# An attention and gated-MLP kernel: batch 0 loaded as rows and transposed on the tensor engine, loads reordered, and the numerators moved one period later

## The chip, the core and the metric

The kernel runs on one core of a Trainium2 chip. A core has a tensor engine (PE, with PEld for its weight loads), a vector engine (DVE), a scalar engine (ACT), GpSimd (POOL) and a sync engine (SP). Each engine works through its own queue of instructions in order and waits on semaphores. DVE and ACT read the tensor engine's results out of PSUM; POOL works in SBUF alone. DMAs are issued by SP, ACT and POOL. The metric is the device time of one execution in microseconds (us).

## The reference

There are B = 8 batches of H = 8 heads, S = 576 positions and D = 64 columns. Attention is linear, with a feature map of 128 columns and their negatives:

```python
proj = np.einsum('bhsd,df->bhsf', x, w_phi)
proj = proj - np.max(np.abs(proj), axis=-1, keepdims=True)
phi = np.concatenate([np.exp(proj), np.exp(-proj)], axis=-1)
kv = np.einsum('bhsf,bhsd->bhfd', k_p, v)
z = np.sum(k_p, axis=2)
num = np.einsum('bhsf,bhfd->bhsd', q_p, kv)
den = np.einsum('bhsf,bhf->bhs', q_p, z)[..., None] + 1e-06
x = num / den
```

The result, as rows of 512 columns, goes through a gated MLP: a causal convolution of five taps gives the gate, and the output is `(sigmoid(gate_pre) * (x @ w_val)) @ w_out`.

## The kernel before

The work goes batch by batch, and each batch is cut into units of one PSUM tile. All PSUM tiles have one tag with four buffers of two banks each (`ps2`), so at most four units are between PE and their readers.

*Loads.* `load_rows` (L70) brings k or q of a batch in transposed: POOL issues a DMA that casts the fp32 rows to bf16 in DRAM (L80, and L85 for the last 64 positions of each head), and SP issues a transposing DMA from there into `KT` or `QT` (L83, L86). `load_v` (L95) brings v in as fp32 rows, `VN` and `VNt`, on SP. `issue_after` places an issue behind a given instruction.

*Stage A, features.* `unit_k` (L210) projects 1024 columns of keys into `PK`; DVE takes the largest absolute value per position (L214), ACT makes the two exponentials `KTIL` (L219), and POOL negates the maxima (L223). `unit_vscale` (L225) makes `EK` from these on ACT (L229), and POOL multiplies v by it (`VT` L234, `VTt` L242, the sum's column L248). `unit_qmax` (L250) projects queries into `PQA` only for their maxima (L254). There are five units of each per batch, the last one half as wide.

*The mark between the stages.* `unit_mrows` (L259) transposes the maxima of q and makes `MQM` (L263), once per batch.

*Stage B.* `unit_qproj` (L268) projects the queries again with the maxima subtracted (`PQ`, L274 and L279), and ACT makes `QTIL` (L284) or, for the tail, `QTILt` (L301). `unit_kv` (L314) multiplies `KTIL` and `VT` into `KVPS` (L324, L334), copied to `KVSB` (L340). `unit_num` (L345) makes numerators and denominators (L355), which DVE divides into `XN` (L362, L364). `unit_xt` (L372) transposes these (L378) into `XT` (L383, L385).

*The MLP.* `unit_gate` (L390) is the convolution as matmuls with the diagonals `DIAG` (L397) and tanh (`GS`, L402), `unit_val` (L404) gives `VAL` (L409) and `GV` (L414), and `unit_out` (L419) gives `OUTp` (L426), which ACT copies to `OUTs` (L432) and SP stores (L440).

*The order.* Batch i's period begins with its stage A, merged by weights with gate and value units of batch i-1 (`merge`, L463). Then comes its stage B, written out by hand (L514 to L535), with the three output units of batch i-1 between. The numerators of batch i stand in its own stage B, behind its kv. So the MLP of a batch is one period behind its features. Batch 0 has its own `first_features` (L477), where `build_diag` (L169) stands behind the casts of q. A scheduler places the instructions of neighbouring units among each other, and each engine keeps the order it gives. The loads of batch i+1 are issued behind the first and second `VT` of batch i (L503, L506).

Of the kernel before, what the change touches and what calls it, by code (L numbers as in the profile page):

```python
# [9 lines left out]
AF = mybir.ActivationFunctionType  # L10
# [3 lines left out]
FP32 = mybir.dt.float32  # L14
BF16 = mybir.dt.bfloat16

B, H, S, D = 8, 8, 576, 64
F = 128
DM = 512
P = 128  # L20
E1 = D + 1
HALF = S // 2
NT = HALF - 2 * P
PAD = 2
TAIL = H * 2 * P
# [8 lines left out]
def kernel(  # L34
# [15 lines left out]
    nc = tc.nc  # L50

    const = ctx.enter_context(tc.tile_pool(name="const", bufs=1))
    dram = ctx.enter_context(tc.tile_pool(name="dram", bufs=3, space=bass.MemoryType.DRAM))
    qtp = ctx.enter_context(tc.tile_pool(name="qtp", bufs=3))
    vnp = ctx.enter_context(tc.tile_pool(name="vnp", bufs=2))
    featp = ctx.enter_context(tc.tile_pool(name="featp", bufs=2))
    smallp = ctx.enter_context(tc.tile_pool(name="smallp", bufs=2))
    vtp = ctx.enter_context(tc.tile_pool(name="vtp", bufs=2))
# [4 lines left out]
    ps2 = ctx.enter_context(tc.tile_pool(name="ps2", bufs=4, space=bass.MemoryType.PSUM))  # L63

    states = [_BatchState() for _ in range(B)]
# [23 lines left out]
    def load_k(st, parts=1):  # L89
        st.KT, st.k_xbars = load_rows(st, k, "KT", parts)  # L90

    def load_q(st, parts=1):
        st.QT, st.q_xbars = load_rows(st, q, "QT", parts)

    def load_v(st, anchor):  # L95
        b = st.b
        st.VN = vnp.tile([P, H, 4, D], FP32, name="VN")
        st.VNt = vnp.tile([P, 2, 2, D], FP32, name="VNt")
        with tc.issue_after(anchor):
            for hh in range(2):  # L100
                nc.sync.dma_start(
                    st.VN[:, 4 * hh:4 * hh + 4, :, :],
                    v[b, 4 * hh:4 * hh + 4, 0:4 * P, :].rearrange("h (p c) d -> p h (c d)", c=4),
                )
            for g in range(2):
                nc.sync.dma_start(
                    st.VNt[:, g, :, :],
                    v[b, 4 * g:4 * g + 4, 4 * P:S, :].rearrange("h (r t) d -> h r (t d)", t=2),
                )

    wtmp = const.tile([P, F], FP32, name="wtmp")
    nc.scalar.dma_start(wtmp[0:D, :], w_phi[:, :])
    nc.scalar.dma_start(wtmp[D:2 * D, :], w_phi[:, :])
    cw5 = const.tile([5, DM], FP32, name="cw5")
# [1 line left out]
    warm = const.tile([P, 1], FP32, name="warm")  # L116
    nc.vector.memset(warm[:, :], 0.0)
    nc.scalar.activation(warm[:, :], warm[:, :], AF.Exp)
    load_k(states[0], 2)


    ident_bf = const.tile([P, P], BF16, name="ident_bf")
# [46 lines left out]
    def build_diag():  # L169
        for dt in range(4):  # L170
            for tap in range(5):
                nc.gpsimd.tensor_scalar_mul(  # L172
                    DIAG[:, dt, tap, :], ident_f[:, :], cwTh[:, dt, tap:tap + 1],
                )

    def load_wval():
        nc.gpsimd.dma_start(WVAL[:, :, :], moe_w_val.rearrange("(dt p) j -> p dt j", p=P))
# [32 lines left out]
    def unit_k(st, u):  # L210
        PK = ps2.tile([P, 2, 4, F], FP32, name="PK", tag="b")
        nx = group_matmuls(st.KT, PK, u, 2)
        sl = slice(8 * u, 8 * u + 2 * nx)
        nc.vector.tensor_reduce(  # L214
            st.MK[:, 1, sl].rearrange("p (x t) -> p t x", t=2), PK[:, :, 0:nx, :],
            AX.X, ALU.max, apply_absolute_value=True,
        )
        for sgn in range(2):
            nc.scalar.activation(  # L219
                st.KTIL[:, sgn, sl, :].rearrange("p (x t) f -> p t x f", t=2),  # L220
                PK[:, :, 0:nx, :], AF.Exp, scale=1.0 - 2.0 * sgn,
            )
        st.neg_ops[u] = nc.gpsimd.tensor_scalar_mul(st.MK[:, 0, sl], st.MK[:, 1, sl], -1.0).ins  # L223
# [26 lines left out]
    def unit_qmax(st, u):  # L250
        PQ = ps2.tile([P, 2, 4, F], FP32, name="PQA", tag="b")
        n = group_matmuls(st.QT, PQ, u, 1)
        with nc.allow_low_precision("bf16 max"):
            nc.vector.tensor_reduce(  # L254
                st.MQb[:, :].rearrange("p (t s) -> p t s", t=2)[:, :, 4 * u:4 * u + n], PQ[:, :, 0:n, :],
                AX.X, ALU.max, apply_absolute_value=True,
            )

    def unit_mrows(st):  # L259
        MQT = ps2.tile([P, P], BF16, name="MQT", tag="b")  # L260
        nc.tensor.transpose(MQT[:, :], st.MQb[:, :], ident_bf[:, :])
        st.MQM = smallp.tile([P, 4, P], BF16, name="MQM")
        nc.vector.tensor_tensor(  # L263
            st.MQM[:, :, :], MQT[:, :].unsqueeze(1).to_broadcast([P, 4, P]),
            MASK[:, :].unsqueeze(2).to_broadcast([P, 4, P]), ALU.mult,
        )
# [152 lines left out]
    def unit_out(st, w):  # L419
        ob = out[st.b].rearrange("(i t) o -> t i o", t=2)  # L420
        cs = (2 * w, 2 * w + 1) if w < 2 else (4,)
        m = P if w < 2 else 2 * NT
        OUTp = ps2.tile([P, 2, DM], FP32, name="OUTp", tag="b")
        for n, c in enumerate(cs):
            for jt in range(4):
                nc.tensor.matmul(  # L426
                    OUTp[0:m, n, :],
                    st.GV[jt][:, :, :].rearrange("p t i -> p (t i)")[:, P * c:P * c + m],
                    WOUT[:, jt, :], start=(jt == 0), stop=(jt == 3),
                )  # L430
        OUTs = mlp.tile([P, 2, DM], FP32, name="OUTs", bufs=4)
        nc.scalar.activation(  # L432
            OUTs[0:m, 0:len(cs), :], OUTp[0:m, 0:len(cs), :], AF.Copy, scale=0.5,
        )
        for n, c in enumerate(cs):
            n0 = P * c
            while n0 < P * c + m:
                par, i0 = n0 // HALF, n0 % HALF
                k = min(P * c + m - n0, HALF - i0)
                nc.sync.dma_start(ob[par, i0:i0 + k, :], OUTs[n0 - P * c:n0 - P * c + k, n, :])  # L440
                n0 += k

    ORDER = (0, 2, 1, 3, 4)
# [5 lines left out]
    def units_features(st):  # L449
        us = []  # L450
        for u in ORDER:
            us.append((1.0, lambda u=u: k_scaled(st, u)))
            us.append((1.0, lambda u=u: unit_qmax(st, u)))
        return us

    def units_valgate(st):
        us = []
        for jt in range(4):
            us.append((1.2, lambda jt=jt: unit_gate(st, jt)))
            us.append((1.0, lambda jt=jt: unit_val(st, jt)))  # L460
        return us

    def merge(ua, ub):  # L463
        ta, tb = sum(w for w, _ in ua) or 1.0, sum(w for w, _ in ub) or 1.0
        ia = ib = 0
        fa = fb = 0.0
        while ia < len(ua) or ib < len(ub):
            if ib >= len(ub) or (ia < len(ua) and fa <= fb):
                fa += ua[ia][0] / ta
                ua[ia][1]()  # L470
                ia += 1
            else:
                fb += ub[ib][0] / tb
                ub[ib][1]()
                ib += 1

    def first_features(st):  # L477
        for u in ORDER:
            unit_k(st, u)
        with tc.issue_after(st.neg_ops[0]):  # L480
            load_q(st, 2)
        load_v(st, st.q_xbars[0])
        with tc.issue_after(st.cast):
            build_diag()
            load_wval()
        for u in ORDER:
            unit_vscale(st, u)
        for u in ORDER:
            unit_qmax(st, u)

    for i in range(B + 1):
        sa = states[i] if i < B else None
        sb = states[i - 1] if i > 0 else None
        if sa:
            alloc_A(sa)
            alloc_B(sa)
        if i == 0:
            first_features(sa)
        else:
            merge(units_features(sa) if sa else [], units_valgate(sb))  # L500
        if i + 1 < B:
            sn = states[i + 1]
            with tc.issue_after(sa.vt_ops[0]):  # L503
                load_k(sn)
            load_v(sn, sn.k_xbars[-1])
            with tc.issue_after(sa.vt_ops[2]):  # L506
                load_q(sn)
                if i == 0:
                    load_wout()
        if not sa:  # L510
            for w in range(3):
                unit_out(sb, w)
            break
        unit_mrows(sa)  # L514
        if sb:
            unit_out(sb, 0)
        unit_qproj(sa, 0)
        unit_kv(sa, 0)
        unit_qproj(sa, 1)
        unit_kv(sa, 1)  # L520
        if sb:
            unit_out(sb, 1)
        unit_qproj(sa, 2)
        unit_num(sa, 0)
        unit_num(sa, 1)
        unit_qproj(sa, 4)
        unit_xt(sa, 0)
        unit_num(sa, 4)
        unit_qproj(sa, 3)
        if sb:  # L530
            unit_out(sb, 2)
        unit_xt(sa, 2)
        unit_num(sa, 2)
        unit_num(sa, 3)
        unit_xt(sa, 1)  # L535


# [28 lines left out]
```

## Time and profile before

| | |
|---|---|
| time, median of 3 runs | 331.03 us (330.91 to 332.42) |
| the profiled execution | 331.03 us, span 329.2 us, mean granted clock 0.965 |
| VT, `VT<-VN` (L234), two of one unit | 2.0 to 2.1 us |
| KTIL (L219), 64 full ones | 1025 ns each |
| maxima (L214), 32 full ones | 1218 ns each |
| OUTs (L432), 16 full ones | 1024 ns each |
| DIAG (L172), 20 on POOL | 11.6 us in all |

The span runs from the first instruction to the last. A line of the timeline gives the start, the duration, engine, source line, operation, result and operand, shapes, the number of instructions merged into it, and in brackets how long the engine had been idle before and what ended the wait. Durations of matmuls contain their latency, so the time from one group's start to the next says more about PE than a mean. The granted clock is 1.00 where PE runs at full speed.

### The profile page before, as it was taken

How to read it: one execution, taken by the hardware profiler on the slowest of the kernel's cores; microseconds unless marked ns; L12 is line 12 of the kernel's file. 1: busy time of each engine (PE TensorE's matmuls, PEld its weight loads, DVE VectorE, ACT ScalarE, POOL GpSimd, SP SyncE). 2: the span in 40 equal slices, each digit the busy share in tenths (PEclk: the TensorE clock that was granted, in tenths of full speed). 3: DMA queues.
4: the chain of work that ended last, by engine and by line, in shares of the span. 5: the costliest groups of instructions: out<-in, count | busy, mean ns of one | idle time of the engine just before them, and what ended most of it. 6: DMA issues, size and time to landing. Idle time of an engine off the chain costs nothing.

```text
span 329.2 us, 7225 instructions
## 1 busy us (share of the span) xinstructions
PE 241.3 (73%) x3053; PEld 151.3 (46%) x3068; DVE 171.4 (52%) x253; ACT 181.8 (55%) x258; POOL 121.8 (37%) x224
## 2 busy tenths in 40 slices
PE   0222585786888787968798878879787887788793
PEld 0211353453555354645455444545454545545471
DVE  2634054482568535781569254872579246854430
ACT  1630364186456683676638663668567663767323
POOL 3499901365005910383034600492037401650000
PEclk9999997699999999999979998999999989999998
DMA  6594299696404792279407881489408970003004
GB/s 114 103 219 67 39 181 227 118 239 132 129 16 70 186 242 82 42 190 219 114 18 135 208 180 55 66 169 223 123 7 143 260 152 16 2 21 109 18 3 143
DMA packets 61834, 39.34 MB, mean 119 GB/s; under 512 B 39653, under 2 KB 53093, under 8 KB 61802
## 3 DMA queue, kind: packets, MB, share of 16 engines
q1 hardware_dynamic: 53888, 28.32, 35.1%
q0 software_dynamic: 7744, 10.49, 19.7%
q8 instruction: 24, 0.39, 0.5%
q10 hardware_dynamic: 170, 0.08, 0.1%
q14 instruction: 8, 0.07, 0.1%
HBM read 30.48 MB, written 18.87 MB: 150 GB/s over the span
## 4 chain that ended last, share of the span: by engine, by line
PE 28%; POOL 22%; DVE 14%; ACT 14%; issue 10%; DMA 6%; SPq 3%; POOLq 0%; ACTq 0%; DVEq 0%
POOL VT L234 12%; PE OUTp L426 8%; DVE MK L214 8%; ACT KTIL L219 5%; ACT QTIL L284 4%; PE NUM L355 4%; PE GATE L397 3%; POOL DIAG L172 3%; PE VAL L409 3%; PE XTP L378 3%; ACT OUTs L432 3%; DVE GV L414 3%; POOL VTt L242 2%; DMA QT<-QTR_342 2%; PE PK L195 2%
## 5 line engine op out<-in xcount | busy, mean ns | idle before, releaser
L219 ACT ACTIVATE KTIL<-PK 128x1024 bf16<-128x1024 f32 (+1 forms) x80 | 70.8, 940 | 47.4 <-DVE MK L214 47.2
L284 ACT ACTIVATE QTIL<-PQ 128x1024 bf16<-128x1024 f32 x64 | 61.7, 1026 | 20.6 <-PE PQ L279 20.6
L223 POOL TENSOR_SCALAR MK<-MK 128x8 f32<-128x8 f32 (+1 forms) x40 | 9.2, 230 | 130.9 <-DVE MK L214 123.9
L397 PE MATMUL GATE<-XT,DIAG 128*128 128x288 bf16 x320 | 47.7, 298 | 7.9 <-DVE XT L383 5.1
L214 DVE TENSOR_REDUCE MK<-PK 128x8 f32<-128x1024 f32 (+1 forms) x40 | 44.2, 1111 | 6.1 <-PE PK L195 6.1
L409 PE MATMUL VAL<-XT,WVAL 128*128 128x288 bf16 x256 | 38.1, 292 | 6.8 <-ACT GS L402 2.0
L426 PE MATMUL OUTp<-WOUT,GV 128*128 128x512 bf16 (+1 forms) x145 | 39.4, 394 | 2.5 <-ACT QTIL L284 1.2
L397 PEld LDWEIGHTS <-DIAG 128*128 128x128 bf16 x320 | 30.9, 100 | 18.8 <-issue 7.0
L340 DVE CAST KVSB<-KVPS 128x520 bf16<-128x520 f32 x16 | 10.7, 697 | 54.9 <-PE KVPS L334 54.9
L432 ACT ACTIVATE OUTs<-OUTp 128x1024 f32<-128x1024 f32 (+1 forms) x24 | 21.0, 878 | 29.4 <-PE OUTp L426 29.4
L402 ACT ACTIVATE GS<-GATE 128x576 bf16<-128x576 f32 x32 | 20.9, 654 | 23.8 <-PE GATE L397 23.8
L414 DVE SCALAR_TENSOR_TENSOR GV<-GS,VAL 128x576 bf16<-128x576 bf16 x32 | 24.0, 751 | 17.0 <-PE VAL L409 12.9
L409 PEld LDWEIGHTS <-WVAL 128*128 128x128 bf16 x256 | 24.1, 99 | 15.8 <-issue 5.0
L254 DVE TENSOR_REDUCE MQB_133<-PQA 128x8 bf16<-128x1024 f32 (+1 forms) x20 | 22.0, 1112 | 10.7 <-PE PQA L195 10.7
L364 DVE TENSOR_TENSOR XN<-NUM,RCP 128x512 bf16<-128x512 f32 (+1 forms) x40 | 26.4, 677 | 0.8
L324 PE MATMUL KVPS<-VT,KTIL 128*128 128x65 bf16 x512 | 21.3, 200 | 7.5 <-POOL VT L248 7.5
L254 DVE TENSOR_REDUCE MQB_135<-PQA 128x8 bf16<-128x1024 f32 (+1 forms) x20 | 22.2, 1112 | 8.3 <-PE PQA L195 8.3
L324 PEld LDWEIGHTS <-KTIL 128*128 128x128 bf16 x512 | 18.6, 101 | 15.2 <-issue 11.7
L195 PE MATMUL PQA<-W_118,QT 64*128 64x128 bf16 x288 | 15.9, 234 | 12.8 <-DMA QT<-QTR_222 5.9
L426 PEld LDWEIGHTS <-GV 128*128 128x128 bf16 (+1 forms) x160 | 14.6, 102 | 18.4 <-issue 6.3
L195 PE MATMUL PK<-W_118,KT 64*128 64x128 bf16 x288 | 17.4, 232 | 7.2 <-ACT KTIL L219 3.0
L378 PE MATMUL XTP<-ident_bf,XN 128*128 128x128 bf16 (+1 forms) x160 | 15.2, 218 | 9.1 <-DVE XN L364 9.1
(194 smaller groups left out, 308.7 us busy)
## 6 DMA issues: line engine op xcount, KB each, us to landing
VN<-in_v_dram SPq DMA_DIRECT2D x16, 512.0 KB
out_dram<-OUTs SPq DMA_DIRECT2D x24, 256.0 KB
out_dram<-OUTs SPq DMA_DIRECT2D x8, 192.0 KB
VNt<-in_v_dram SPq DMA_DIRECT2D x16, 64.0 KB
out_dram<-OUTs SPq DMA_DIRECT2D x8, 128.0 KB
KTRt<-in_k_dram POOLq DMA_DIRECT2D x8, 64.0 KB, 2.5
QTRt<-in_q_dram POOLq DMA_DIRECT2D x8, 64.0 KB, 5.4
WVAL<-in_moe_w_val_dram POOLq DMA_DIRECT2D x1, 512.0 KB, 5.4
```

The costliest lines, as they stand in the source:

```text
L195: nc.tensor.matmul(PS[:, par, x, :], T[ROWS[par], cols], W2[ROWS[par], :], start=True, stop=True,)
L214: nc.vector.tensor_reduce(st.MK[:, 1, sl].rearrange("p (x t) -> p t x", t=2), PK[:, :, 0:nx, :], AX.X, ALU.max, apply_absolute_value=True,)
L219: nc.scalar.activation(st.KTIL[:, sgn, sl, :].rearrange("p (x t) f -> p t x f", t=2), PK[:, :, 0:nx, :], AF.Exp, scale=1.0 - 2.0 * sgn,)
L234: st.vt_ops[u] = nc.gpsimd.tensor_tensor(st.VT[:, sgn, sl, 0:D].rearrange("p (x t) d -> p x t d", t=2), st.VN[:, 4 * hh:4 * hh + 4, 2 * jj ...
L254: nc.vector.tensor_reduce(st.MQb[:, :].rearrange("p (t s) -> p t s", t=2)[:, :, 4 * u:4 * u + n], PQ[:, :, 0:n, :], AX.X, ALU.max, apply_a ...
L284: nc.scalar.activation(st.QTIL[:, sgn, u, :, :, :], PQ[:, :, :, :], AF.Exp, scale=1.0 - 2.0 * sgn,)
L324: nc.tensor.matmul(KVPS[:, xi, c0:c0 + E1], st.KTIL[:, sgn, s, :], st.VT[:, sgn, s, :], start=(g == 0 and sgn == 0 and jp == 0), stop=Fals ...
L397: nc.tensor.matmul(GATE[:, par, 0:HALF], DIAG[:, jt, tap, :], XT[:, jt, t % 2, i0:i0 + HALF], start=(tap == 0), stop=(tap == 4),)
L409: nc.tensor.matmul(VAL[:, par, 0:HALF], WVAL[:, dt, jt * P:(jt + 1) * P], XT[:, dt, par, PAD:PAD + HALF], start=(dt == 0), stop=(dt == 3),)
L414: nc.vector.scalar_tensor_tensor(out=st.GV[jt][:, :, :], in0=GS[:, :, :], scalar=1.0, in1=VAL[:, :, 0:HALF], op0=ALU.add, op1=ALU.mult,)
L426: nc.tensor.matmul(OUTp[0:m, n, :], st.GV[jt][:, :, :].rearrange("p t i -> p (t i)")[:, P * c:P * c + m], WOUT[:, jt, :], start=(jt == 0), ...
L432: nc.scalar.activation(OUTs[0:m, 0:len(cs), :], OUTp[0:m, 0:len(cs), :], AF.Copy, scale=0.5,)
```

## The change

Batch 0's k and q come in as fp32 rows, on SP, without a cast and without a transposing DMA; PE transposes them in fp32 into PSUM and ACT and DVE copy them, as bf16, to `KT` and `QT`. The loads of batch 1 and its v follow, and those of the MLP weights come in the period of batch 1. The diagonals are built where the code of batch 0's k features ends. The numerators of a batch move into stage B of the next batch, ahead of that batch's kv and between its projections. The whole MLP of a batch, output units too, is merged into the feature stage two batches later. So the loop has one more turn at the end. The pool of `KT` and `QT` has two buffers where it had three, and that of `VN`, which now holds k and q of batch 0 as well, has three where it had two.

```diff
-    qtp = ctx.enter_context(tc.tile_pool(name="qtp", bufs=3))
-    vnp = ctx.enter_context(tc.tile_pool(name="vnp", bufs=2))
+    qtp = ctx.enter_context(tc.tile_pool(name="qtp", bufs=2))
+    vnp = ctx.enter_context(tc.tile_pool(name="vnp", bufs=3))
+    def load_natural(st, src, name, eng):
+        b = st.b
+        N = vnp.tile([P, H, 4, D], FP32, name="VN")
+        Nt = vnp.tile([P, 2, 2 * D], FP32, name=name + "t")
+        for hh in range(2):
+            eng.dma_start(
+                N[:, 4 * hh:4 * hh + 4, :, :],
+                src[b, 4 * hh:4 * hh + 4, 0:4 * P, :].rearrange("h (p c) d -> p h (c d)", c=4),
+            )
...
+    def transpose_natural(N, Nt, T, hp, copy):
+        TP = ps2.tile([P, 2, 2, 2, P], FP32, name="TP", tag="b")
+        if hp < 4:
+            for x in range(2):
+                for jj in range(2):
+                    nc.tensor.transpose(
+                        TP[:, 0, x, jj, :],
+                        N[:, 2 * hp + x, 2 * jj:2 * jj + 2, :].rearrange("p t d -> p (t d)"), ident_f[:, :],
+                    )
+            copy(
+                T[:, 4 * P * hp:4 * P * hp + 4 * P].rearrange("q (x i j) -> q x j i", x=2, j=2),
+                TP[:, 0, :, :, :],
+            )
...
+    K0 = load_natural(states[0], k, "K0", nc.sync)
-    load_k(states[0], 2)
+    with tc.issue_after(K0[2]):
+        Q0 = load_natural(states[0], q, "Q0", nc.sync)
     def first_features(st):
-        for u in ORDER:
-            unit_k(st, u)
-        with tc.issue_after(st.neg_ops[0]):
-            load_q(st, 2)
-        load_v(st, st.q_xbars[0])
-        with tc.issue_after(st.cast):
-            build_diag()
-            load_wval()
+        st.KT = qtp.tile([P, H * HALF], BF16, name="KT")
+        st.QT = qtp.tile([P, H * HALF], BF16, name="QT")
+        load_v(st, Q0[2])
+        for hh in range(2):
+            transpose_natural(K0[0], K0[1], st.KT, 2 * hh, act_copy)
+            transpose_natural(K0[0], K0[1], st.KT, 2 * hh + 1, nc.vector.tensor_copy)
+            unit_k(st, hh)
+            unit_k(st, 2 + hh)
+        transpose_natural(K0[0], K0[1], st.KT, 4, act_copy)
+        unit_k(st, 4)
+        build_diag()
...
+        with tc.issue_after(st.neg_ops[1]):
+            load_k(states[1])
+            load_q(states[1])
+        load_v(states[1], states[1].q_xbars[-1])
         for u in ORDER:
             unit_vscale(st, u)
-        for u in ORDER:
-            unit_qmax(st, u)
+    def units_mlp(st):
+        return units_valgate(st) + [(1.8, lambda w=w: unit_out(st, w)) for w in range(3)]
...
+    for i in range(B + 2):
...
-            merge(units_features(sa) if sa else [], units_valgate(sb))
+            merge(units_features(sa) if sa else [], units_mlp(sc) if sc else [])
...
-                if i == 0:
+                if i == 1:
+                    load_wval()
                     load_wout()
...
+        num = units_num(sb) if sb else []
+        if sa:
+            unit_mrows(sa)
+            kv = units_kv(sa)
+            merge(units_q(sa), num[0:3] + kv[0:1] + num[3:6] + kv[1:2] + num[6:])
+        else:
+            merge([], num)
```

In the diff `sa` is batch i, `sb` batch i-1 and `sc` batch i-2.

## The prediction

> **What bounds the kernel now.** I read the page first, then the busy time by engine in stretches, then the timeline. The page:
>
> ```profile
> span 329.2 us, 7225 instructions
> PE 241.3 (73%) x3053; PEld 151.3 (46%) x3068; DVE 171.4 (52%) x253; ACT 181.8 (55%) x258; POOL 121.8 (37%) x224
> PE 28%; POOL 22%; DVE 14%; ACT 14%; issue 10%; DMA 6%; SPq 3%; POOLq 0%; ACTq 0%; DVEq 0%
> ```
>
> No engine is full, and the chain that ended last passes from engine to engine: the bound is order and waiting. MQM (L263) runs once per batch, between the feature stage and the stage of query projections, kv and numerators, so the timeline of VectorE gives the periods:
>
> ```profile
> 27.83 0.69 DVE L263 TENSOR_TENSOR MQM<-MQT,MASK 128x512 bf16<-128x512 bf16 x1 [0.38 <-PE MQT L261]
> 75.53 0.69 DVE L263 TENSOR_TENSOR MQM<-MQT,MASK 128x512 bf16<-128x512 bf16 x1 [0.33 <-PE MQT L261]
> 112.12 0.69 DVE L263 TENSOR_TENSOR MQM<-MQT,MASK 128x512 bf16<-128x512 bf16 x1 [0.32 <-PE MQT L261]
> 255.62 0.69 DVE L263 TENSOR_TENSOR MQM<-MQT,MASK 128x512 bf16<-128x512 bf16 x1 [0.33 <-PE MQT L261]
> 292.25 0.69 DVE L263 TENSOR_TENSOR MQM<-MQT,MASK 128x512 bf16<-128x512 bf16 x1 [0.33 <-PE MQT L261]
> ```
>
> Batch 0 to 1 takes 47.7 us, the six periods after it (292.25 - 75.53) / 6 = 36.1 each, and 37.0 follow the last mark. Busy time by stretch (columns: stretch, its length, PE, PEld, DVE, ACT, POOL, granted clock, DMA share, GB/s): a stall in the head; one stage B (mark to the next GATE); one stage A (GATE to the mark); the last mark to the last GATE group; the end.
>
> ```profile
> 54.00:60.00 6.00, 2.76 (x18) 1.44 (x16) 0.80 (x1) 2.58 (x4) 3.03 (x5) 0.50 1.08 203
> 220.32:239.37 19.05, 15.54 (x245) 9.37 (x246) 7.89 (x17) 11.06 (x15) 3.59 (x8) 1.00 0.75 183
> 239.37:255.62 16.25, 13.03 (x137) 8.67 (x137) 13.22 (x14) 11.38 (x18) 9.74 (x17) 1.00 0.45 78
> 292.25:310.48 18.23, 15.21 (x237) 9.06 (x237) 7.92 (x16) 10.93 (x13) 1.04 (x2) 1.00 0.21 67
> 310.48:329.20 18.72, 13.45 (x91) 8.74 (x92) 3.02 (x4) 5.20 (x7) 0.00 (x0) 0.94 0.19 64
> ```
>
> PE idles 3.5 us in stage B and 3.2 in stage A: together it works 28.6 of 35.3. The timeline of the head:
>
> ```profile
> 15.76 11.62 POOL L172 TENSOR_SCALAR DIAG<-ident_f,cwTh 128x128 bf16<-128x128 f32 x20
> 28.18 2.05 POOL L234 TENSOR_TENSOR VT<-VN,EK_258 128x512 bf16<-128x512 f32 x2
> 42.90 0.70 DVE L340 CAST KVSB<-KVPS 128x520 bf16<-128x520 f32 x1 [2.69 <-PE KVPS L334]
> 53.72 2.56 PE L397 MATMUL GATE<-XT,DIAG 128*128 128x288 bf16 x10 [0.62 <-DVE XT L383]
> 59.52 0.61 PE L195 MATMUL PQA<-W_118,QT 64*128 64x128 bf16 x8 [3.24 <-DMA QT<-QTR_342]
> ```
>
> POOL builds the 20 diagonals, only then scales v of batch 0, and kv waits for it; then batch 1's q is late, and PE falls to half clock.
>
> **The change, part by part.** The profiled execution is at 331.03 us, the median, so the sum is against its own span: 329.2 + 1.8.
>
> **1. Batch 0 as fp32 rows.** Gone are its six POOL casts and six SP transposes; new are eight loads of k and q on SP, ahead of v's four, 36 PE transposes and 10 copies (ACT 6, DVE 4). A copy of 512 columns costs 0.62 on ACT by QTILt (L301, 620 ns) and 0.70 on DVE by KVSB (697 ns). An fp32 transpose of 128 columns isn't in the trace: at least 0.10 by the bf16 XTP rows (four in 0.40), at most 0.63 by the longest 512-column PQ matmul; I take 0.2, as the 5-column fp32 ones of cw cost 0.14. Landing isn't shown for SP loads: wtmp, issued at 0.72, let DVE start at 5.08; 512 KB at the busiest slice's 260 GB/s is 2 us. So half of k lands near 6.5 and all of it near 8.5. ACT's program has the copies of both halves ahead of the first KTIL, which starts at 8.5 + 8 x 0.2 + 0.62 = 10.7, against 10.88 now. Nothing is gained in k; ends 9 and 14.
>
> On POOL all 20 DIAG now stand ahead of the five MK negations: from cwTh (6.5 now, a little later with big loads beside it) they run 7 to 18.7, the negations to 19.4. ACT's queue has EK ahead of the first copy of QT, so it waits with them: EK 19.7, the tail's KTIL 20.8, QT copy 21.4. Then in turn two qmax (2 x 1.22), the DVE copy 0.70, three more reductions (3.1) and hand-overs: the mark falls at 30, two later than 27.83 (ends 27.5 and 33). On POOL follow four casts for batch 1 (2.4), VT for two units from 22.3, and VTt; the other two EK stand behind the first QTIL pair (30.9 to 33), so VT ends at 33.4 + 4.3 = 37.7. Kv of batch 0 has 76 matmuls left then, and 85 take some 5 now with projections between (37.56 to 42.85): 4, and the rest of the projections 1.2. The features of batch 1 start at 43, against 52.2, since batch 0's numerators are gone from between.
>
> **2. Batches 1 and 2.** Batch 1 is cast from about 20 and its transposes are done before 40: the 3.24 wait for QT goes. Its feature stage has no MLP in it; DVE sets it with ten reductions (8 x 1.22 + 2 x 0.68 = 11.1) plus 1.2 of start: mark at 55.3, against 75.53. What is late next: ACT has two EK behind all KTIL (54.6), POOL's VT and VTt then end at 60.4, and kv of batch 1 waits for that (1.7). Behind them on POOL stand the cast of q of batch 2 and the weight loads, from 60.6: by QT_342 (cast 5 to 7, transpose 6.6 from issue, 52.89 to 59.5) QT lands near 73, where PE wants it at 71.7; WVAL (issued at 62, 5.4 alone, q's cast beside it) lands in time for 70.7. So 1.3 us. Mark of batch 2: 55.3 + 33.0 + 1.7 + 1.3 = 91.3, against 112.12; ends 85 (nothing late) and 102 (q as late as now, and a stage at half clock).
>
> **3. The period.** OUT moves from stage B to A: 39.4 / 8 = 4.9 us of PE, 21.0 / 8 = 2.6 of ACT. Stage A with its idle kept is 16.25 + 4.9 = 21.1; I take 20.9. Stage B loses this and, as numerators now belong to the batch before, the waits at its end (XTP for XN 0.86, XT for XTP 0.55, GATE for XT 0.62) and NUM's for QTILt (0.86): 19.05 - 4.9 - 2.9 = 11.3; kv's copy, XT and XN then share DVE closer together, so 12.1. Period 33.0; ends 30.5 (PE's 28.6 and half a wait per stage) and 36.1 (the idle comes back). Five periods, batch 2 to 7: 165 against 180.1. The old ones hide nothing of this: each ends at the mark.
>
> Casts and transposes of later batches are issued as early as now; SP has the six stores of the batch before ahead of the last VNt and QT transposes, and these still land some 7 us before use. The buffer counts cost nothing: with two, QT's next buffer was last read a whole period before, and k, q and v of batch 0 have VN's three to themselves.
>
> **4. The tail.** Behind the last mark: stage B 12.1; MLP of batch 6 alone, as at 310.48 to 323.98, 13.5; numerators of batch 7, on DVE 5 x 0.90 + 2 x 0.69 + 0.29 = 6.2 and 1.3 of hand-overs, 7.5; MLP of batch 7, 18.7 as now. Sum 51.8, against 37.0: +14.8. It was cover in the last period before, and is bare now. Ends 48 and 55.
>
> Sum: 91.3 + 165 + 51.8 = 308.1; with 1.8, **310**.
>
> **Rules weighed.** The clock fell to 0.50 behind PE's idle before 59.52, and ten GATE matmuls then took 2.56 where 1.39 is usual. [...]
>
> **The rivals.**
> *The idle comes back.* PK holds one of four PSUM buffers through one reduction and two exponentials (1.22 + 2 x 1.03), and 21 tiles share them in stage A where there were 18. The period stays 36.1: 310 + 5 x 3.1 = 325. For it: the waits of KTIL for MK, 47.2 in all. Against: those are ACT's, not PE's.
> *More goes.* Period 30.5: 310 - 12.5 = 297. For it: ACT and DVE are below 60%. Against: PE alone then works 17.9 in stage A and 10.6 in B.
> *Slower.* In stage A each OUT tile's buffer waits on ACT behind a KTIL pair (2.05): three of these put 6.2 on the period, 39.2, and the time is 341. It decides from 33.0 + 21 / 5 = 37.2 on. For it: ACT's program has OUTs behind KTIL. Against: OUT needs no ACT to start, and ACT has 16.25 - 11.4 = 4.9 free there now.
> *The first load gains nothing at all*, batch 1 marking at 62: 317, inside my own range.
>
> **How the numbers follow.** 0.5% (1.7 us) is about what a measurement of this kernel can tell from no change. Forecast, 303 to 317: 0.57. Idle back, 317 to 329: 0.17. More goes, under 303: 0.12. Within 0.5%: 0.03. Slower: 0.11. So faster 0.86. 298 leaves 0.03 below; 327 leaves 0.03 of the second case and the last two above, 0.17.
>
> **What would show it.** MQM marks near 30, 55, 91, then every 33; no PE wait for QT in the head; DIAG on POOL from 7; stage B near 12, stage A near 21; 52 behind the last mark. It is wrong if marks stay 36 apart, if SP loads of 3.5 MB land after 20, or if kv waits for VT in every period.

## The result and the profile after

The changed kernel takes 305.16 us (median of four, 304.15 to 305.54), the kernel before 331.73 beside it (330.91 to 332.42). The ratio is 0.9195, with an interval of 0.9158 to 0.9232: 8% faster. The prediction said 310. The profiled execution took 304.15, span 302.3. Line numbers are now those of the changed kernel (MQM is L300). The page:

```profile
span 302.3 us, 7310 instructions
PE 247.7 (82%) x3096; PEld 158.9 (53%) x3104; DVE 178.0 (59%) x257; ACT 185.7 (61%) x264; POOL 119.5 (40%) x218
PE 69%; DVE 15%; ACT 5%; DMA 5%; issue 3%; POOL 1%; ACTq 0%
```

PE is busy 6 us longer than before (the 36 transposes alone are 8.8: four groups of eight at 1.97, two of two at 0.44) and is now 82% busy. The chain that ended last runs on PE for 69% of the span where it was 28%, and on POOL for 1% where it was 22%. The timeline of VectorE gives the marks; mark n is the MQM of batch n:

```profile
30.48 0.69 DVE L300 TENSOR_TENSOR MQM<-MQT,MASK 128x512 bf16<-128x512 bf16 x1 [0.38 <-PE MQT L298]
54.51 0.69 DVE L300 TENSOR_TENSOR MQM<-MQT,MASK 128x512 bf16<-128x512 bf16 x1 [0.38 <-PE MQT L298]
93.83 0.69 DVE L300 TENSOR_TENSOR MQM<-MQT,MASK 128x512 bf16<-128x512 bf16 x1 [0.32 <-PE MQT L298]
125.04 0.69 DVE L300 TENSOR_TENSOR MQM<-MQT,MASK 128x512 bf16<-128x512 bf16 x1 [0.32 <-PE MQT L298]
...
250.98 0.69 DVE L300 TENSOR_TENSOR MQM<-MQT,MASK 128x512 bf16<-128x512 bf16 x1 [0.32 <-PE MQT L298]
```

Mark 2 falls 18.3 us earlier than before (93.83 for 112.12). The five periods from there on take 157.15 where they took 180.13, which is 23.0 less. The end, behind the last mark, takes 51.3 where it took 36.9, which is 14.4 more. That makes 26.9, the difference of the two spans.

Busy time by stretch, with the columns of the prediction: a stage B, a stage A, and the one period of five that was longer than 31.2.

```profile
156.25:168.87 12.62, 10.88 (x226) 7.59 (x225) 8.11 (x17) 9.33 (x13) 3.34 (x5) 1.00 0.92 235
168.87:187.46 18.59, 17.27 (x158) 10.27 (x159) 13.66 (x15) 13.18 (x20) 10.10 (x19) 1.00 0.60 96
187.46:219.78 32.32, 29.73 (x384) 18.51 (x383) 21.61 (x31) 22.51 (x33) 13.45 (x24) 0.95 0.75 166
```

PE idles 1.7 us in stage B and 1.3 in stage A, where it idled 3.5 and 3.2. The timeline of the head, with the lines that answer to those of before:

```profile
7.28 1.97 PE L133 MATMUL TP<-ident_f,VN 128*128 128x128 f32 x8
7.75 11.98 POOL L209 TENSOR_SCALAR DIAG<-ident_f,cwTh 128x128 bf16<-128x128 f32 x20 [6.02 <-DVE MASK L188]
33.69 0.22 ACT L266 ACTIVATE EK_383<-MK 128x16 f32<-128x16 f32 x1
33.99 2.04 POOL L271 TENSOR_TENSOR VT<-VN,EK_383 128x512 bf16<-128x512 f32 x2 [5.49 <-ACT EK_383 L266]
70.39 2.40 PE L434 MATMUL GATE<-XT,DIAG 128*128 128x288 bf16 x10 [0.16 <-DVE XT L422]
76.56 0.40 PE L232 MATMUL PQA<-W_120,QT 64*128 64x128 bf16 x8 [2.11 <-DMA QT<-QTR_696]
76.88 2.08 PE L434 MATMUL GATE<-XT,DIAG 128*128 128x288 bf16 x10
```

The diagonals are built early; VT of batch 0 stops for 5.49 us until the third EK; q of batch 1 is in time, and now q of batch 2 is late, by 2.11; the ten GATE matmuls ahead of that wait take 2.40, and the ten behind it 2.08, where 1.41 is usual.

### The profile page after: what moved, and what is told of

It reads as the page before. It is cut to its first block, busy times and chain, and to the rows that moved or that the text cites. A ratio compares the mean times of both kernels' runs of the same rounds, so it can differ in the third digit from the quotient of the medians.

```text
span 302.3 us, 7310 instructions
## 1 busy us (share of the span) xinstructions
PE 247.7 (82%) x3096; PEld 158.9 (53%) x3104; DVE 178.0 (59%) x257; ACT 185.7 (61%) x264; POOL 119.5 (40%) x218
## 3 DMA queue, kind: packets, MB, share of 16 engines
HBM read 30.48 MB, written 17.69 MB: 159 GB/s over the span
## 4 chain that ended last, share of the span: by engine, by line
PE 69%; DVE 15%; ACT 5%; DMA 5%; issue 3%; POOL 1%; ACTq 0%
PE GATE L434 12%; PE OUTp L463 12%; PE VAL L446 10%; PE KVPS L361 6%; PE NUM L392 6%; DVE XN L401 4%; PE XTP L415 4%; ACT KTIL L256 4%; PE PQ L316 4%; DVE MK L251 4%; PE PQA L232 3%; PE PQ L311 3%; DMA QT<-QTR_696 3%; PE PK L232 3%; DVE MQB_137 L291 2%
## 5 line engine op out<-in xcount | busy, mean ns | idle before, releaser
L439 ACT ACTIVATE GS<-GATE 128x576 bf16<-128x576 f32 x32 | 20.9, 652 | 39.5 <-PE GATE L434 39.5
L446 PE MATMUL VAL<-XT,WVAL 128*128 128x288 bf16 x256 | 39.1, 297 | 0.0
L463 PE MATMUL OUTp<-WOUT,GV 128*128 128x512 bf16 (+1 forms) x152 | 38.0, 382 | 0.4
L291 DVE TENSOR_REDUCE MQB_135<-PQA 128x8 bf16<-128x1024 f32 (+1 forms) x20 | 22.1, 1116 | 14.4 <-PE PQA L232 14.3
L446 PEld LDWEIGHTS <-WVAL 128*128 128x128 bf16 x256 | 25.1, 102 | 8.8 <-issue 0.2
L401 DVE TENSOR_TENSOR XN<-NUM,RCP 128x512 bf16<-128x512 f32 (+1 forms) x40 | 27.6, 690 | 1.4
L361 PE MATMUL KVPS<-VT,KTIL 128*128 128x65 bf16 x512 | 22.8, 203 | 2.5 <-POOL VT L285 2.5
L361 PEld LDWEIGHTS <-KTIL 128*128 128x128 bf16 x512 | 20.4, 103 | 7.8 <-issue 6.9
L463 PEld LDWEIGHTS <-GV 128*128 128x128 bf16 (+1 forms) x160 | 13.7, 100 | 17.1 <-DVE GV L451 2.6
L392 PEld LDWEIGHTS <-QTIL 128*128 128x128 bf16 x512 | 18.1, 100 | 7.4 <-issue 7.4
```

The source lines that it names most:

```text
L291: nc.vector.tensor_reduce(st.MQb[:, :].rearrange("p (t s) -> p t s", t=2)[:, :, 4 * u:4 * u + n], PQ[:, :, 0:n, :], AX.X, ALU.max, apply_a ...
L361: nc.tensor.matmul(KVPS[:, xi, c0:c0 + E1], st.KTIL[:, sgn, s, :], st.VT[:, sgn, s, :], start=(g == 0 and sgn == 0 and jp == 0), stop=Fals ...
L392: nc.tensor.matmul(NUM[0:m, g, x * E1:(x + 1) * E1], lhsT, st.KVSB[:, x, g, sgn, :], start=(sgn == 0), stop=(sgn == 1),)
L401: nc.vector.tensor_tensor(XN[0:m, :, :].rearrange("p (g x) d -> p g x d", g=2), NUMv[:, :, :, 0:D], RCP[0:m, :, :].unsqueeze(3).to_broadca ...
L446: nc.tensor.matmul(VAL[:, par, 0:HALF], WVAL[:, dt, jt * P:(jt + 1) * P], XT[:, dt, par, PAD:PAD + HALF], start=(dt == 0), stop=(dt == 3),)
L463: nc.tensor.matmul(OUTp[0:m, n, :], st.GV[jt][:, :, :].rearrange("p t i -> p (t i)")[:, P * c:P * c + m], WOUT[:, jt, :], start=(jt == 0), ...
```

## The experiments

Times are medians. Ratios are to the kernel before, measured on the same chip in the same series.

| what runs | us | ratio (95% interval) | mark 1 | mark 2 | last mark | span |
|---|---|---|---|---|---|---|
| before | 331.73 | 1 | 75.53 | 112.12 | 292.25 | 329.2 |
| changed | 305.16 | 0.9195 (0.9158 to 0.9232) | 54.51 | 93.83 | 250.98 | 302.3 |
| loads alone | 327.01 | 0.9846 (0.9774 to 0.9919) | 70.26 | 105.56 | 285.47 | 322.4 |
| order alone | 313.19 | 0.9415 (0.9362 to 0.9468) | 69.20 | 101.98 | 258.00 | 311.1 |
| output units alone | 329.01 | 0.9894 (0.9828 to 0.9959) | 75.27 | 111.98 | 292.99 | 328.0 |
| numerators alone | 318.29 | 0.9607 (0.9503 to 0.9712) | 69.30 | 99.56 | 261.23 | 315.4 |
| changed, 3 PSUM buffers | 333.23 (one run) | | 59.87 | 101.77 | 277.92 | 331.5 |
| changed, diagonals late | 308.22 | 0.9247 (0.9185 to 0.9309) | 56.30 | 98.16 | 255.31 | 306.7 |
| changed, q of batch 2 early | 299.35 | 0.8990 (0.8922 to 0.9058) | 53.39 | 88.45 | 245.61 | 297.0 |
| changed, v of batch 0 first | 303.52 | 0.9110 (0.9053 to 0.9167) | 52.13 | 92.81 | 248.84 | 301.7 |
| both of these | 296.11 | 0.8892 (0.8832 to 0.8951) | 52.14 | 85.67 | 242.81 | 294.1 |
| both, extra matmuls in the head | 296.79 | 0.8940 (0.8862 to 0.9018) | 52.90 | 85.07 | 241.07 | 294.1 |
| q of batch 2 early, four EK buffers | 294.03 | 0.8826 (0.8780 to 0.8872) | 51.58 | 84.15 | 240.15 | 291.5 |

### The loads alone

```diff
-        for u in ORDER:
-            unit_k(st, u)
-        with tc.issue_after(st.neg_ops[0]):
-            load_q(st, 2)
+        for hh in range(2):
+            transpose_natural(K0[0], K0[1], st.KT, 2 * hh, act_copy)
...
+        with tc.issue_after(st.neg_ops[1]):
+            load_k(states[1])
+            load_q(states[1])
             load_wval()
+            load_wout()
```

> The loads alone: batch 0 as fp32 rows, batch 1 early, weights behind it, but the order of before in every period (numerators of a batch in its own stage B, three output units in stage B). My theory, that the two parts act in different places and add up: mark 0 near 30.5 as in the changed kernel, mark 1 near 69.5 (batch 0's numerators still stand ahead of batch 1's features, but the wait for q of batch 1 is gone) against 75.5 before, then six periods of 36.1 and 37 behind the last mark: 325 us, 6 to 7 us less than before. Rival, that batch 0's scaled v or its numerators hold the head anyway: mark 1 at 75 and 331 us. Rival, that most of the gain was in the loads: 310 us or less.

Marks at 30.57 and 70.26, six periods in 215.2 (35.9 each), 36.9 behind the last mark: span 322.4, 6.8 less than before. (This is the profiled execution, the shortest of four; the ratio in the table makes it 5.) The theory's 325 lies among the runs (324.14, 326.57, 327.45 and 329.12). Neither rival holds.

### The order alone

```diff
+    for i in range(B + 2):
...
+            merge(units_features(sa) if sa else [], units_mlp(sc) if sc else [])
...
+        num = units_num(sb) if sb else []
+        if sa:
+            unit_mrows(sa)
+            kv = units_kv(sa)
+            merge(units_q(sa), num[0:3] + kv[0:1] + num[3:6] + kv[1:2] + num[6:])
```

> The order alone: numerators one batch later, the whole MLP merged into the feature stage two batches later, with the loads, casts, diagonals and buffer counts of before. My theory: q of batch 1 lands as late as before (59.5), so mark 1 falls near 67, mark 2 near 101, then five periods of 31.4 as in the changed kernel and 51.3 behind the last mark: 309 to 314 us, so 18 to 22 us less than before; with the loads alone (6 to 7 less) this makes the whole of the 27. Rival, that the order needs the early loads (features without MLP beside them run at half clock while q is late, and later batches' loads stay behind): periods above 33 and 320 us or more.

313.19, with marks at 69.20 and 101.98 and then 31.20 per period, as in the changed kernel: the order needs nothing of the loads. What the loads are for shows in the timeline of PE in this kernel:

```profile
51.86 0.61 PE L230 MATMUL PK<-W,KT 64*128 64x128 bf16 x8 [8.00 <-DMA KT<-KTR]
58.96 0.60 PE L230 MATMUL PQA<-W,QT 64*128 64x128 bf16 x8 [6.49 <-DMA QT<-QTR]
```

Freed of batch 0's numerators, PE gets to batch 1's features at 43.9 and then waits 8.00 for k and 6.49 for q. Neither part alone brings mark 1 forward by more than 6.3 us (69.20 and 70.26 for 75.53); together they bring it to 54.51, by 21.0. Most of that is given back by mark 2, though, so that in the span the parts are nearly additive: 6.8 and 18.1 make 24.9, both together 26.9.

### The output units alone, and the numerators alone

The order has two parts, so each was run by itself beside the loads of before. Output units in stage A, numerators where they were:

```diff
-            merge(units_features(sa) if sa else [], units_valgate(sb))
+            merge(units_features(sa) if sa else [], units_mlp(sb))
...
         unit_mrows(sa)
-        if sb:
-            unit_out(sb, 0)
```

> One part of the order alone: the three output units of a batch go from the hand-written stage B into the merge with the next batch's features; numerators stay in their own batch's stage B, loads as before. My theory, that the numerators' own waits (for the kv copy, for QTILt, XN and XT) are what the order took out of stage B: with the output units gone, stage B has even less to put between them, so that it stays near 15.5 while stage A becomes 19 to 20: period 34.5 to 35.5, time 321 to 327 us. Rival, that it was the output units standing in stage B that cost: period 31.4 as in the changed kernel, 303 us. Rival, that nothing is gained without both: 331 us.

And numerators in the next batch's stage B, the three output units left in stage B:

```diff
+            merge(units_features(sa) if sa else [],
+                  (units_valgate(sc) if sa else units_mlp(sc)) if sc else [])
...
+            o = units_mlp(sc)[-3:] if sc else []
+            merge(units_q(sa),
+                  o[0:1] + num[0:3] + kv[0:1] + num[3:6] + o[1:2] + kv[1:2] + num[6:] + o[2:3])
```

> The fourth corner beside the loads of before: numerators one batch later, among the projections of the next stage B (as in the changed kernel), but the three output units kept in stage B. With the order of before the period is 36.1, with the output units alone in stage A it was 36.3 in the mean and 35.3 where the clock did not fall, with both moves 31.2. Theory, that it is the numerators which matter, since in their own batch's stage B they wait for the kv copy, QTIL, XN and XT with nothing beside them: period 31.5 to 33.5, 313 to 325 us. Rival, that neither move does much alone because stage A without the output units is set by DVE's ten reductions and four GV (about 16): period 34 to 36, 325 to 333 us.

With the loads of before, the mean period from mark 2 to the last mark is 36.0 with neither part, 36.2 with the output units moved, 32.3 with the numerators moved, 31.2 with both. It is mainly the numerators: moving them takes off 3.7, or 5.0 where the output units are moved too; moving the output units adds 0.2 alone and takes off 1.1 beside the numerators. (Moving the numerators also puts the MLP one batch later and replaces the hand-written order of stage B by a merge; no run separates these.) The output units alone gave 329.01, worse than the 321 to 327 expected. Busy time by stretch of that kernel, one stage B and the stage A behind it, and the first GATE group between them from the timeline:

```profile
183.99:200.07 16.08, 12.22 (x226) 8.22 (x225) 7.97 (x17) 9.23 (x13) 3.36 (x6) 0.96 0.72 173
200.07:220.76 20.69, 19.84 (x158) 11.29 (x158) 13.58 (x15) 13.18 (x20) 9.99 (x18) 0.86 0.67 132
```

```profile
200.07 2.56 PE L397 MATMUL GATE<-XT,DIAG 128*128 128x288 bf16 x10 [0.56 <-DVE XT L383]
```

As expected, stage B keeps its waits: PE idles 3.9 of 16.1. What was not expected is the clock. It fell in each of this kernel's six periods (granted 0.91 to 0.95 in the mean of a period), and the first GATE group took 2.56 us in each, for 1.41 at full clock. The periods at 0.95 took 35.3 and 35.5, those at 0.91 36.7 to 36.8. So some of what the move freed went into half clock; how much, no run separates.

The same stretches with the numerators moved and the output units kept:

```profile
131.58:147.38 15.80, 14.64 (x244) 9.21 (x245) 7.97 (x16) 11.01 (x15) 3.63 (x7) 1.00 0.84 210
147.38:163.59 16.21, 13.08 (x141) 8.79 (x138) 13.37 (x15) 11.76 (x19) 9.76 (x18) 1.00 0.54 82
```

Stage B went from 19.05 to 15.80 with as many units of each kind in it: PE now idles 1.2 there. Stage A is as before, 16.21 with 3.1 idle. Moving the output units as well takes 3.2 from stage B (to 12.62) and puts only 2.4 on stage A (to 18.59), although they are 4.2 us of PE's work there (17.27 for 13.08): they fill stage A's waits. The order alone and the changed kernel have the same two stages to 0.01 us.

### A PSUM buffer less

```diff
-    ps2 = ctx.enter_context(tc.tile_pool(name="ps2", bufs=4, space=bass.MemoryType.PSUM))
+    ps2 = ctx.enter_context(tc.tile_pool(name="ps2", bufs=3, space=bass.MemoryType.PSUM))
```

> The changed kernel with three PSUM buffers of two banks in place of four. It prices the rival 'the idle comes back' of the prediction: if PE's waits in stage A are for a buffer that a reduction and two exponentials still read, a buffer less makes a period clearly longer, by 3 to 8 us (time 325 to 360 us). If four are more than enough, as a stage A of 18.7 us with 17 us of work would have it, the period stays within 1 us and the time under 312 us.

333.23, with periods of 35.2, 4.0 longer, at full clock. What PE waits for in one of them (137.00 to 172.23; total, times, longest):

```profile
PE OUTp L463 <- ACT KTIL L256: 1.5, 2, 1.1
PE PQA L232 <- ACT KTIL L256: 0.8, 1, 0.8
PE GATE L434 <- DVE GV L451: 0.6, 1, 0.6
```

These waits for a buffer are what two of the prediction's rivals feared: output tiles behind KTIL, tiles behind a reduction. None of the three is there with four buffers; one of the kind is left, GATE for KTIL, 0.5. So the rivals' mechanism is real: with three buffers it costs the whole gain, with four little of it is left.

### The diagonals late

```diff
-        build_diag()
...
+        with tc.issue_after(st.vt_ops[3]):
+            build_diag()
```

> The changed kernel with the 20 diagonals built behind batch 0's last VT in place of ahead of the negations. The prediction put two microseconds of mark 0 and the late VT down to the diagonals standing first on POOL. Theory of the prediction: negations, EK and the first copy of QT go earlier by 1 to 2 us, mark 0 near 29, VT of batch 0 ends near 36, time 302 to 303 us. Rival, which the profile of the changed kernel speaks for (ACT reaches EK only at 19.98, when the negations are already done at 19.71): ACT's own order sets mark 0, which stays at 30 to 30.5, VT of batch 0 still ends near 38 since two EK stand behind QTIL, and the diagonals then hold POOL from 38 to 50, ahead of batch 1's negations and VT, so that batch 1's kv comes 2 to 6 us later: 305 to 311 us.

308.22, and mark 0 at 30.94 in place of 30.48: the diagonals did not hold it. In the changed kernel POOL negates the first maxima at 19.71 and ACT, behind eight KTIL and a copy, comes to EK at 19.98; with POOL free, EK still ran only at 19.94. The prediction's reason for mark 0 is wrong, and building the diagonals early is worth 4.3 us at mark 2 (93.83 for 98.16). The timelines of POOL and of PE, late diagonals:

```profile
38.88 11.63 POOL L209 TENSOR_SCALAR DIAG<-ident_f,cwTh 128x128 bf16<-128x128 f32 x20
50.48 0.45 POOL L260 TENSOR_SCALAR MK<-MK 128x8 f32<-128x8 f32 x2
```

```profile
79.91 0.61 PE L232 MATMUL PQA<-W,QT 64*128 64x128 bf16 x8 [4.26 <-DMA QT<-QTR]
```

Batch 1's negations wait for them on POOL until 50.48, and so do its VT and, behind these in POOL's queue, the cast of q of batch 2, which is then late by 4.26.

### q of batch 2 early, v of batch 0 first, and both

q of batch 2 a period earlier:

```diff
+            if i == 1:
+                load_q(states[2])
             merge(units_features(sa) if sa else [], units_mlp(sc) if sc else [])
```

> The changed kernel with the loads of q of batch 2 issued one period earlier, right behind batch 0's VT, so that QT of batch 2 is there when its feature stage wants it. It prices the term of 1.3 us for q of batch 2 being late (in the profile of the changed kernel PE waited 2.11 for it, and 10 GATE matmuls before and after took 2.40 and 2.08 where 1.41 is usual). Theory: the wait goes and with it part of the half clock, mark 2 at 89 to 92 in place of 93.8, all later marks by as much: 300 to 303 us. Rival, that the transfer only moves the wait to k of batch 2, whose transposes now stand behind: 305 us or more.

299.35. The wait is gone, and the GATE and VAL groups of this stage run at full clock, 1.41 and 1.15 from the first on. Mark 2 is at 88.45, 5.4 earlier. The stage began 0.5 earlier (GATE at 69.87 for 70.39); the wait was 2.1, and the GATE and VAL groups on either side of it, which had taken 2.40, 1.86, 2.08 and 1.83, were 3.0 longer than at full clock. Not all of the 3.0 can be put down to the late q. Busy time by stretch in the changed kernel:

```profile
67.21:70.62 3.41, 2.24 (x59) 1.70 (x55) 2.32 (x6) 1.42 (x3) 0.00 (x0) 1.00 1.19 193
70.62:74.03 3.41, 3.41 (x17) 2.14 (x16) 0.95 (x1) 2.43 (x4) 0.53 (x2) 0.50 1.27 144
74.03:77.44 3.41, 1.30 (x16) 0.78 (x15) 0.45 (x1) 0.15 (x1) 2.48 (x4) 1.00 0.97 106
77.44:80.86 3.42, 3.42 (x22) 1.90 (x21) 2.67 (x3) 0.70 (x2) 0.00 (x0) 0.50 0.80 146
```

The first spell at half clock began at 70.62, and PE came to the wait for q only at 74.45. So 1.7 of the 3.0 ran ahead of the wait, and the late q cost its 2.1 and some 1.3 behind it. With q early the first spell is gone as well; no run shows why.

EK and VT of batch 0 traced ahead of its q units, diagonals behind them:

```diff
+        with tc.issue_after(st.neg_ops[1]):
+            load_k(states[1])
+            load_q(states[1])
+        load_v(states[1], states[1].q_xbars[-1])
+        for u in ORDER:
+            unit_vscale(st, u)
         for hh in range(2):
             transpose_natural(Q0[0], Q0[1], st.QT, 2 * hh, act_copy)
...
+        with tc.issue_after(st.vt_ops[3]):
+            build_diag()
```

> The changed kernel with batch 0's EK and VT traced ahead of its q units (so that no EK stands behind QTIL on ACT) and with the diagonals behind VT. It tests the step that VT of batch 0, ending at 38.5, is what kv of batch 0 and so the start of batch 1's features (43.0) wait for. Theory: VT ends near 33, batch 1's features start at 38 to 40, mark 1 at 50 to 52 and the time is 299 to 303 us. Rival, that something else is late by as much (diagonals on POOL ahead of batch 1's VT, or batch 1's loads): marks from 2 on unchanged, 305 us or more.

303.52: VT of batch 0 ended at 32.5 in place of 38.5 and mark 1 came 2.4 earlier, but mark 2 only 1.0. The timeline of PE behind mark 1:

```profile
69.41 1.85 PE L446 MATMUL VAL<-XT,WVAL 128*128 128x288 bf16 x8 [2.05 <-DMA WVAL<-in_moe_w_val_dram]
74.71 0.61 PE L232 MATMUL PQA<-W,QT 64*128 64x128 bf16 x8 [3.44 <-DMA QT<-QTR]
```

The time lies between the theory's range (up to 303) and the rival's (from 305 on), but the mechanism is the rival's: PE is earlier and waits longer for the value weights and for q, whose loads stand behind batch 1's VT. With q taken out of that queue the gain comes through:

> The last two together: batch 0's v scaled first, diagonals behind it, and q of batch 2 a period earlier. If both are separate losses in the head they add up: mark 2 at 86 to 89, 295 to 300 us. If they are two faces of one limit (POOL's work and its casts up to batch 2), it is no better than the better one alone, 300 to 303 us.

296.11, mark 2 at 85.67: 8.2 earlier, where the two alone gave 5.4 and 1.0. They are not two separate losses but one behind the other: the earlier start is worth something only where q is there.

### Holding the clock in the head

```diff
+        for n in range(extra):
+            nc.tensor.matmul(
+                PS[:, n % 2, :, :], ident_bf[:, :], EB[:, 0:4, :], start=True, stop=True,
+            )
```

> The version with batch 0's v scaled first and q of batch 2 early, with two extra matmuls of 512 columns ahead of every feature tile of batch 1 and every query tile of batch 0; their results are written over by the real ones, so the computation stays whole. They fill PE's idle time in the head, where the granted clock was 0.50 from 18 to 38 and 0.50 to 0.63 from 45 to 56. Theory, that the clock follows PE's idle: it stays near 1.00 from the middle of the head on, the 12 us of work that ran at half speed behind mark 0 and mark 1 take 4 to 6 us less, of which VT hides half: mark 2 at 83 to 84 in place of 85.7, time 293 to 295 us. Rival, that the extra matmuls do not hold the clock, or that their own 10 us on PE lie on the path: mark 2 at 86 or later, 296 us or more.

Busy time by stretch, first without and then with the extra matmuls:

```profile
18.00:38.00 20.00, 12.65 (x119) 8.15 (x119) 8.81 (x10) 7.43 (x16) 17.09 (x28) 0.50 0.75 167
45.00:56.00 11.00, 6.30 (x75) 4.19 (x75) 9.05 (x12) 9.90 (x17) 9.93 (x18) 0.54 0.97 169
```

```profile
24.00:48.00 24.00, 16.70 (x240) 9.60 (x237) 16.23 (x16) 13.73 (x19) 23.64 (x39) 0.98 0.54 118
48.00:56.00 8.00, 6.36 (x59) 2.91 (x57) 4.08 (x7) 6.45 (x12) 6.90 (x14) 0.57 1.02 177
```

The clock was held from 24 to 48 (0.98), in which PE is 70% busy, and lost again (0.57 from 48 to 56) behind a wait of 2.13. Mark 2 moved from 85.67 to 85.07, the span not at all (294.1 both): the time is 296.79 for 296.11, no difference. The equal spans are in part chance. At the last mark the extra matmuls are 1.7 ahead, 1.1 of it because the kernel without them has a spell at half clock in its last period (GATE at 223.09 takes 2.45); behind that mark they take 53.0 for 51.3, with a spell of their own (GATE at 253.68 takes 2.56). The half clock of the head cost next to nothing in this pair: what PE does there waits in any case for VT of batch 1, which ended at 58.3 and 58.9, and in both the clock was back by 56.0 (1.00 from 56 to 60). What the extra matmuls cost on PE is in this result too, and no run separates it.

The same run has the transposes at both clocks, at 0.50 (18 to 24) and, with the second group, in the stretch at 0.98 (24 to 48):

```profile
20.13 1.97 PE L133 MATMUL TP<-ident_f,VN 128*128 128x128 f32 x8
24.70 1.19 PE L133 MATMUL TP<-ident_f,VN 128*128 128x128 f32 x8
```

### Four buffers for EK

The last trace left one question: why the third EK is late. In the changed kernel it stood behind QTIL on ACT; with v first it waited, on ACT again, for the first VT. Both go back to a pool of two buffers.

```diff
-        EK = smallp.tile([P, 2, 2 * nx], FP32, name=f"EK{nx}")
+        EK = smallp.tile([P, 2, 2 * nx], FP32, name=f"EK{nx}", bufs=4)
```

> The version with only q of batch 2 early, and one argument more: four buffers for EK in place of two. In the changed kernel the third and fourth EK of batch 0 run at 33.69, behind the first QTIL, and VT waited 5.49 for them; the version that scales v first had them wait for the first two VT instead (2.36 and 1.92 on ACT), so it is the two buffers that hold them, and ACT's queue only shows it. Theory: with four, all EK run by 23, VT of batch 0 runs through from 23 to 33 with no wait, the diagonals stay ahead of it where they cost nothing, batch 1's features start near 39 to 40, mark 1 near 51, mark 2 at 84 to 86.5 in place of 88.45: 294 to 297 us. Rival, that kv of batch 0 then waits for QTIL on ACT, or that batch 1's VT on POOL sets mark 2: mark 2 stays within 1 us of 88.45 and the time at 298.5 us or more.

294.03, the lowest time of all (its interval still touches that of "both of these"), 11.7% under the kernel before. The timelines of ACT, POOL and VectorE:

```profile
19.52 0.62 ACT L266 ACTIVATE EK<-MK 128x16 f32<-128x16 f32 x3
22.34 0.31 ACT L266 ACTIVATE EK<-MK 128x16 f32<-128x16 f32 x2
```

```profile
22.72 2.05 POOL L271 TENSOR_TENSOR VT<-VN,EK 128x512 bf16<-128x512 f32 x2
...
29.15 2.04 POOL L271 TENSOR_TENSOR VT<-VN,EK 128x512 bf16<-128x512 f32 x2
```

```profile
51.58 0.69 DVE L300 TENSOR_TENSOR MQM<-MQT,MASK 128x512 bf16<-128x512 bf16 x1 [0.38 <-PE MQT L298]
84.15 0.69 DVE L300 TENSOR_TENSOR MQM<-MQT,MASK 128x512 bf16<-128x512 bf16 x1 [0.32 <-PE MQT L298]
```

All EK have run by 22.7, VT goes through without a stop and ends at 32.5, batch 1's features start at 40.2, and mark 2 is 9.7 us earlier than in the changed kernel. From there on all five periods are 31.2.

## Why the prediction was right, step by step

| step | predicted | measured |
|---|---|---|
| mark 0 | 30 | 30.5 |
| VT of batch 0 ends | 37.7 | 38.5 |
| batch 1's features start | 43 | 43.0 |
| mark 1 | 55.3 | 54.5 |
| VT of batch 1 ends | 60.4 | 60.4 |
| mark 2 | 91.3 | 93.8 |
| stage B | 12.1 | 12.6 |
| stage A | 20.9 | 18.6 |
| five periods | 165 | 157.2 |
| behind the last mark | 51.8 | 51.3 |
| span | 308.1 | 302.3 |

**The head** came out as the prediction laid it out, with one step right for the wrong reason. An fp32 transpose took 0.25 (eight in 1.97), not 0.2; this was at half speed (granted 0.50 at 20.44), and in the stretch at 0.98 of the run with extra matmuls eight took 1.19, 0.15 each. Mark 0 was put two microseconds late because the diagonals stand first on POOL; late diagonals left mark 0 where it was, and ACT's own queue set it. That the other EK stand behind QTIL was right by position; the cause is their two buffers. The timeline of the kernel before shows it already, with the third EK waiting for POOL's first VT and no QTIL ahead of it:

```profile
30.45 0.21 ACT L229 ACTIVATE EK_268<-MK 128x16 f32<-128x16 f32 x1 [10.87 <-POOL VT L248]
```

**Batch 2** is the first mis-sized term: 1.3 us for q being late. The cast was issued at 60.3, as predicted, but q landed at 76.5 and not 73: the cast took 6.7, inside the 5 to 7 assumed, and the transposing DMA, issued at 67.13, some 9.4 where 6.6 was taken. The wait was 2.1, and the groups around it ran at half clock for another 3.0, of which 1.7 came ahead of the wait. From mark 1 to mark 2 it took 39.3, which is 8.1 over the steady 31.2; the prediction allowed 3.0 over its period, and that period, 1.8 too long, hid part of the miss.

**The period** is the second, and the larger: 7.9 us too long in five. Stage A was summed "with its idle kept", 3.2 us. The output units filled the waits instead, and 1.3 were left; their work was 4.2 and not 4.9. The numerators' waits in stage B were put at 2.9, and moving the numerators alone took 3.25 from that stage. Half clock is a smaller part that the prediction did not count: in the last five periods before, three had a granted clock of 0.95 and took 36.5 to 36.6, the others 35.3; after, one of five (32.3 for 31.2).

**The tail** was within 0.5 us, and term by term: 12.6, 13.4, 6.7 and 18.6 for the 12.1, 13.5, 7.5 and 18.7 of the sum. The cover that the MLP and numerators had in the last period was bare, and 14.4 us were paid for it once, as predicted.

The mechanism was right, and two sizes were off in opposite directions: mark 2 came 2.5 late, the five periods 7.9 short. That the total missed by only 5 us is partly luck.

**The rivals.** "The idle comes back" and the slower case did not come, and the runs show how near they were: with three PSUM buffers the period is 35.2 and the gain gone. "More goes" named a period of 30.5; it was 31.2 wherever the clock held, and the head's lateness kept the time at 305. That the first load gains nothing was priced at mark 1 at 62: it was 54.5, and without the early loads 69.2.

**The clock.** Two readings of the kernel before don't hold. The prediction has the clock fall behind PE's wait for q, and ten GATE matmuls then taking 2.56. But that group started at 53.72 and the clock on record fell at 53.74, ahead of this wait (56.28 to 59.52). Nor was PE at full clock through the first 43 us of that head. The record of the clock begins with its first change, at 43.51 before and at 12.60 in the changed kernel; earlier the views read 1.00, yet the matmuls ran at half speed. 32 KVPS matmuls took 1.94 at 40.36, as they did with 0.50 granted (changed kernel, 60.27), and 1.17 at full clock (before, 294.41). So the mean of 0.965 given for the kernel before is too high.

In the changed kernel the clock was 0.50 from 16.0 to 26.2, from 29.7 to 43.3 and from 46.7 to 63.8: stage B of batch 1 began at half clock, for which the prediction's sum has no term. Up to 60.4 this cost nothing that shows, since kv waited for VT. From there to 63.8 PE worked without a break at half clock. The stage took 15.9 (54.51 to 70.39) where later ones take 12.6, and no run separates what of the 3.3 is VT's and what the clock's; in the pair of runs with and without extra matmuls the clock was back before VT was there, so they don't price it. Around the wait for q half clock cost the 3.0 named above.

What makes the clock fall is not shown. In the kernel with the output units alone it fell in all six periods (0.91 to 0.95 granted in the mean), although no wait of PE in the one from 220.76 to 256.27 was over 0.9 us. In the changed kernel PE was busy 2.24 us from 196.92 to 200.33 and the clock fell, and 2.24 us from 166.20 to 169.61 and it did not. So in the one it fell without a long wait of PE, and in the other the busy time does not tell the two places apart. The spells at 0.50 in the changed kernel lasted from 3.41 us (70.62 to 74.03, 200.33 to 203.74) to 17.07 (46.73 to 63.80).

Nor is it shown what the transposes do to the clock. From 9.18 to 12.60, where the changed kernel's record begins with 1.00, PE was busy 3.19 us, 2.03 of it with transposes; no run separates these from the matmuls between them.

## What to carry to other kernels

Work that waits for its own stage's results belongs one period later, where all it needs is already there: here that took 3 us from every period and cost its cover once, at the end. Work moved into a stage that has idle time costs less than its length (here 4.2 us of PE's work put 2.4 on stage A), so its idle must not be added on top, as long as the buffers reach. When a wait is gone, look for what is late next, load by load: scaling v of batch 0 first was worth 1 us at mark 2 until q of batch 2 came earlier too, and a small pool (two EK buffers) held up the head through a queue that seemed to be the reason.

## What the runs showed of the hardware

- fp32 transposes of 128 columns follow the clock: with extra matmuls eight took 1.97 us at 20.13, with 0.50 granted (18 to 24), and 1.19 at 24.70, in a stretch at 0.98 (24 to 48). In the changed kernel single ones took 0.42 at 0.50 (20.44) and 0.27 to 0.33 at 1.00 (26.4). A bf16 GATE group of ten took 2.56 (before, 53.72) and 1.41 at full clock.
- In steady loops too the clock fell to 0.50 for a while. Three periods with a mean of 0.95 took 1.1 to 1.4 us longer than those beside them at 1.00: 32.32 for 31.21 (changed kernel, with 0.50 from 200.33 to 203.74), 36.63 for 35.30 (before), 33.45 for 32.02 (numerators alone).
- Ahead of the first change on record the views read 1.00 while PE ran at half speed; the time of a known group of matmuls tells (32 KVPS: 1.94 at 40.36 of the kernel before, as with 0.50 granted at 60.27 of the changed one; 1.17 at 1.00, 294.41 before).
- With extra matmuls the granted clock was 0.98 from 24 to 48, with PE 70% busy, where it was 0.50 from 18 to 38 without them, and the time did not change (296.79 for 296.11).
